# Block 0: conversions on ScalarE queued behind the Silu of an earlier chunk

## The chip, the cores and the metric

The kernel runs on one core of one Trainium2 chip. The metric is device time of one execution in microseconds; the kernel before took 980.23 us (median of 3 runs, 980.2 to 981.69). A core has five instruction queues that run in order each: TensorE (PE in the rows), VectorE (DVE), ScalarE (ACT), GpSimd (POOL) and SyncE (SP), which here issues the transfers. An instruction that waits holds up everything behind it in its own queue.

## The reference

```python
attn = softmax(scale * q @ k.T, masked)          # 4 batches, 8 heads, 576 positions, head size 64
                                                 # heads 0-3: the last 32 positions; heads 4-7: every 32nd
x = (attn @ v)  -> [2304, 512]
xn = x / sqrt(mean(x * x) + 1e-6) * rms_g
x = (silu(xn @ w_gate) * (xn @ w_val)) @ w_out   # [512,1536], [512,1536], [1536,512]
out = ((x @ w_a) * (x @ w_b)) @ w_out2           # the same sizes, other weights
```

All inputs and outputs are float32. Products are made as three matmuls on a high and a low part of each operand (hi*hi + hi*lo + lo*hi), so that every weight has to be converted into such a pair once, and every activation too.

## The kernel before, in words

The 2304 tokens are worked in six blocks of 384 (`t` = 0 to 5), and the hidden width of 1536 in twelve chunks of 128 (`fc` = 0 to 11). For each block and chunk, PE makes `g` and `v` (12 matmuls each, lines 478 to 480, of the block's normalised attention output `xx` with the chunk's pair `gv`), DVE scales `g` (line 750, tile `sg`), ACT applies Silu to it (line 751), DVE multiplies with `v` (line 761, tile `h`), ACT and POOL (or DVE) split `h` into its pair `hl` (lines 502 and 503), and one chunk later PE adds `h` times the output weights into four accumulators `y` (12 matmuls, same lines). `g` and `v` share three PSUM banks in turn. Block t+1's attention is worked between the chunks of block t: DVE and POOL make the strided heads (POOL products at lines 245 and 278, DVE sums at 248 and 281), and PE, ACT and DVE the local heads.

Block 0 has more to do: the weights come as raw 64-bit words and are converted here, chunk by chunk, one conversion being two steps on ACT (lines 134 and 139), one on DVE (142), a copy to the high part on ACT (147) and a subtraction for the low part on POOL (148). `convert1(fc + 1)` makes the gate and value weights of the next chunk (tiles `gv_raw`, `cz`, `gv`); another conversion, behind line 765, makes the output weights of this chunk (`raw` or `gv_raw`, a half as large `cz`, `wo`), which are then stored to DRAM (`wod`, line 767) for the blocks after. The small `cz` of the output weights has one buffer, so the next conversion's second step waits until POOL has made the low part of the one before. Chunk 11's gate and value words, and the output words of chunks 8 to 11, pass through a pool of two `raw` buffers (`load_late`): a load waits for DVE to have read what was in the buffer.

The order on each engine is not written out. The framework's scheduler lays instructions out by a timeline of its own and keeps data dependences; the source says only what may not be moved ahead of what: inside `with gate(n)` (lines 590 to 596) everything stays behind some steps of block 0's attention on the same engine, and `behind(list)` (lines 493 to 498), so far used for the last block, keeps what is traced inside it behind each listed instruction on the engine of that instruction.

Of the kernel before, what the change touches and what calls it, by code (L numbers as in the profile page):

```python
# [14 lines left out]
AF = mybir.ActivationFunctionType  # L15
# [59 lines left out]
def fused_kernel(ctx: ExitStack, tc: tile.TileContext, qtl, ktl, vl, qs, ks, vs, cst, w1, w2, out):  # L75
# [5 lines left out]
    nc = tc.nc  # L81

    def engine(c):
        return {"P": nc.gpsimd, "D": nc.vector}[c]
# [65 lines left out]
    def conversion(third, ready, pool, lo_eng, low, out=False):  # L150

        st = {}
        n = ready.shape[1] // 2

        def z():
            if not st:
                st["z"] = pool.tile([128, (1 if out else 2) * DM], U32, tag=f"cz{out}", name="cz", bufs=NCZ[out])
            return st["z"][:, :n * DM]

        def last():  # L160
            x = z().bitcast(F32).rearrange("p (a n) -> p a n", a=n)
            hl = ready.rearrange("p (a s) n -> p a s n", s=2)
            parts(x, hl[:, :, 0], hl[:, :, 1], lo_eng)

        return words(third, z, low=low) + [last]

    def run(steps):
        for f in steps:
            f()
# [312 lines left out]
    def mm_in(ps, w, sel, x):  # L482
        for cc in range(NCC):
            c = slice(cc * 128, (cc + 1) * 128)
            mm3(ps, w[:, sel, 0, c], w[:, sel, 1, c], x[cc][:, 0], x[cc][:, 1], cc == 0, cc == NCC - 1)

    def tmp(name):
        return act.tile([128, NTB], F32, tag="t", name=name, bufs=NTMP)

    made = []  # L490

    @contextmanager
    def behind(instructions):

        with ExitStack() as e:
            for i in instructions:
                e.enter_context(tc.issue_after(i))
            yield

    def split(h, lo_eng):  # L500
        hl = act.tile([128, 2, NTB], F32R, tag="hl", name="hl", bufs=3)
        made.append(nc.scalar.copy(hl[:, 0], h).ins)  # L502
        made.append(lo_eng.tensor_tensor(hl[:, 1], h, hl[:, 0].bitcast(F32), op=ALU.subtract).ins)  # L503
        return hl
# [26 lines left out]
    def load_units(n):  # L531
        for which in units[:n]:
            raw.update(zip(which, load_pair(w1, which)))
        del units[:n]

    def load_late(which):
        raw.update(zip(which, load_pair(w1, which, pool)))

    def convert1(fc):
        t = gv[fc] = gv_slot(F32R, "gv")  # L540
        two = [raw.pop((fc, k)) for k in range(2)]
        if fc in FUSEDW:
            both, ready = gvraw[fc], t.rearrange("p k a n -> p (k a) n")
            run(conversion(both.rearrange("p k a n -> p (k a) n"), ready, pool, engine(WLO[fc][0]), LOW[fc][0]))
        else:
            run(zipped(*(conversion(two[k], t[:, k], pool, engine(WLO[fc][k]), LOW[fc][k]) for k in range(2))))

    def wo_tile():
        return wop.tile([128, 2, DM], F32R, tag="wo", name="wo", bufs=3)
# [27 lines left out]
    @contextmanager  # L577
    def gate(fc):

        with ExitStack() as e:  # L580
            for key in GATES[min(fc, len(GATES) - 1)].split():
                e.enter_context(tc.issue_after(s0["st"][key].ins))
            yield
# [7 lines left out]
    def emit_y(t, fc):  # L591
        if fc == 0:
            for e in range(NCC):
                y[t, e] = psum.tile([128, 512], F32, tag=f"y{e}", name=f"y{e}")
        h = hl.pop((t, fc))
        w = wo.pop((t, fc))
        for e in range(NCC):
            c = slice(e * 128, (e + 1) * 128)
            mm3(y[t, e][:, :NTB], w[:, 0, c], w[:, 1, c], h[:, 0], h[:, 1], fc == 0, fc == NFC - 1)

    def evac_y(t):
        for e in range(NCC):
            ys = tmp("ys")
            nc.vector.tensor_tensor(ys, y[t, e][:, :NTB], ri[t], op=ALU.mult)
            nc.sync.dma_start(x2d[t, e // 2][:, e % 2], ys)

    def load_wo(t, fc):
        wt = wo[t, fc] = wo_tile()
        nc.sync.dma_start(wt.rearrange("p a n -> p (a n)").bitcast(F32), wod[fc])
# [4 lines left out]
    def attention_slot(steps, fc):  # L614
        st = steps["strided"]
        n_sl = 10
        part = st[len(st) * fc // n_sl:len(st) * (fc + 1) // n_sl] if fc < n_sl else []
        part += local[min(t, 1)].get(fc, "").split()
        part += ["rms", "rinv"] * (fc == n_sl)
        for n in part:  # L620
            steps[n]()
# [98 lines left out]
    for t in range(NB):  # L720
        if t == 1:
            apool.close()
            pool = apool.enter_context(tc.tile_pool(name="attn", bufs=1))
        if t == NB - 1:
            apool.close()
            cpool.close()
            pool = p2.enter_context(tc.tile_pool(name="forms", bufs=1, reuse_waits="tile"))
            early = [f for k in (4, 5, 0, 1, 2, 3) for f in convert_forms(k, k < 4)]
        nxt = attention(t + 1, pool, psum, itertools.cycle(["att"])) if t + 1 < NB else None
        x = [xt[t, cc] for cc in range(NCC)]  # L730
        for fc in range(NFC):
            if t > 0 and fc == 0:
                load_wo(t, 0)
            g_ps = psum.tile([128, 512], F32, tag="gv", name="g_ps", bufs=3)
            mm_in(g_ps[:, :NTB], gv[fc], 0, x)
            v_ps = psum.tile([128, 512], F32, tag="gv", name="v_ps", bufs=3)
            mm_in(v_ps[:, :NTB], gv[fc], 1, x)
            if t == 0 and fc + 1 < NFC:
                with gate(fc + 1):
                    convert1(fc + 1)  # L740
                if fc + 2 == NFC:
                    load_late([(NFC - 2, 2), (NFC - 1, 2)])
            if t == NB - 1:
                slab[fc] = wgt.tile([128, 4 * DM], F32 if fc in (0, 1, 11) else F32R, tag="gv", name="slab", bufs=NFC)
                with behind(made):
                    run(early[len(early) * fc // NFC:len(early) * (fc + 1) // NFC])
                    for k in [k for k in x0 if k <= fc]:
                        run(x0.pop(k))
            sg = tmp("sg")
            nc.vector.tensor_tensor(sg, g_ps[:, :NTB], ri[t], op=ALU.mult)  # L750
            nc.scalar.activation(sg, sg, AF.Silu)  # L751
            if fc == 1 and t > 0:
                evac_y(t - 1)
            if nxt is not None:
                attention_slot(nxt, fc)
            if prev is not None:
                emit_y(*prev)
            if t > 0 and fc + 1 < NFC:
                load_wo(t, fc + 1)
            h = tmp("h")  # L760
            made[:] = [nc.vector.tensor_tensor(h, sg, v_ps[:, :NTB], op=ALU.mult).ins]  # L761
            hl[t, fc] = split(h, engine(HLO0[fc] if t == 0 else HLO[t]))
            if t == 0:
                wt = wo[0, fc] = wo_tile()
                with gate(fc + 1):
                    run(conversion(raw.pop((fc, 2)), wt, pool, engine(WLO[fc][2]), LOW[fc][2], True))
                nc.sync.dma_start(wod[fc], wt.rearrange("p a n -> p (a n)").bitcast(F32))
                if fc % 2:
                    load_units(1)
                if fc == NFC - 3:  # L770
                    load_late([(NFC - 1, 0), (NFC - 1, 1)])
            prev = (t, fc)
# [240 lines left out]
```

## Time and profile before

| | |
|---|---|
| median of the runs | 980.23 us |
| profiled execution | 981.02 us |
| its span on the core | 979.2 us |
| PE busy | 949.2 us, 97% |
| DVE, ACT, POOL busy | 63%, 44%, 57% |
| mean granted clock of PE | 0.986 |

The span is from the first instruction to the last; 1.8 us of the profiled execution lie around it. PE has 30 us in which it does nothing, most of them in the first 160 us: the attention of block 0 up to 35 us, block 0's chunks from there to about 140 us. Matmuls of 384 columns start 0.17 us after each other at the full clock and overlap, so that a duration of 0.33 us is two of them. A row of the timeline gives the start, the busy time, the instruction, and in brackets how long its engine was idle before it and what ended that.

### The profile page before, as it was taken

The page shows a single profiled execution, that of the slowest core. Times are in us where ns is not written, and L with a number is a line of the kernel's source. Part 1 is how long each engine was busy: PE and PEld are TensorE (multiplying, and loading weights), DVE is VectorE, ACT ScalarE, POOL GpSimd, SP SyncE. Part 2 cuts the span into 40 slices and gives each one's busy share as a digit, 9 for nine tenths or more (in the row PEclk, how much of TensorE's full clock was granted, in tenths as well). Part 3 has the DMA queues.
Part 4 walks back from the last instruction along what each step waited for, and adds up shares of the span by engine and source line. Part 5 has one row for each costly group of instructions (what it writes and reads, how often), then busy time and mean ns, then how long its engine had stood idle before and what let it go on. Part 6 is the DMA issues. An engine that isn't in the chain of part 4 may idle for free.

```text
span 979.2 us, 14353 instructions
## 1 busy us (share of the span) xinstructions
PE 949.2 (97%) x5438; PEld 900.8 (92%) x5438; DVE 620.4 (63%) x891; ACT 427.7 (44%) x800; POOL 555.1 (57%) x418
## 2 busy tenths in 40 slices
PE   6899999999999999999999899999999999999998
PEld 5799989999999999999999899999999999999996
DVE  5568757638917984988565458667655655465534
ACT  4999645243534423433456455535434423122110
POOL 3489946558739776969468644754743424123211
PEclk7899999999999999999999999999999999999999
DMA  9963375435633643532687975897893973853701
GB/s 339 408 238 119 117 284 206 147 111 178 191 110 126 208 161 107 175 121 80 217 328 278 374 284 209 330 419 312 325 386 122 351 305 117 295 233 150 269 11 65
DMA packets 57364, 215.57 MB, mean 220 GB/s; under 512 B 5968, under 2 KB 14544, under 8 KB 51664
## 3 DMA queue, kind: packets, MB, share of 16 engines
q1 hardware_dynamic: 57296, 214.66, 59.7%
q8 instruction: 43, 0.70, 0.3%
q14 instruction: 25, 0.20, 0.1%
HBM read 172.17 MB, written 42.47 MB: 219 GB/s over the span
## 4 chain that ended last, share of the span: by engine, by line
PE 75%; DVE 6%; DMA 5%; POOL 5%; ACT 4%; issue 3%; SPq 1%; DVEq 0%; POOLq 0%; ACTq 0%
PE o L892 5%; PE o L894 5%; PE o L893 5%; PE Y L838 4%; PE Y L837 4%; PE Y L836 4%; PE y L478 3%; PE g_ps L478 3%; PE v_ps L478 3%; PE g_ps L480 3%; PE v_ps L480 3%; PE g_ps L479 3%; PE v_ps L479 3%; PE y L479 3%; PE y L480 3%
## 5 line engine op out<-in xcount | busy, mean ns | idle before, releaser
L148 POOL TENSOR_TENSOR hl<-c,hl 128x384 fp32r<-128x384 f32 x72 | 77.9, 1082 | 180.5 <-ACT hl L147 173.9
L245 POOL TENSOR_TENSOR prod<-kv_t,qs_t 128x512 f32<-128x512 f32 (+12 forms) x57 | 106.1, 1883 | 18.3 <-DMA kv_t<-in_ks 6.3
L503 POOL TENSOR_TENSOR hl<-h,hl 128x384 fp32r<-128x384 f32 x70 | 77.9, 1113 | 59.7 <-ACT hl L502 59.7
L478 PE MATMUL g_ps<-xx,gv 128*128 128x384 f32 x288 | 98.4, 342 | 5.1 <-DVE h L761 5.0
L478 PE MATMUL v_ps<-xx,gv 128*128 128x384 f32 x288 | 97.5, 339 | 3.5 <-DVE sg L750 3.0
L278 POOL TENSOR_TENSOR prod<-kv_t,S_t 128x512 f32<-128x512 f32 (+12 forms) x57 | 86.0, 1522 | 24.0 <-DVE S_t L270 7.7
L479 PE MATMUL y<-hl,wo 128*128 128x384 f32 x288 | 96.8, 341 | 1.3 <-POOL hl L503 1.3
L479 PE MATMUL v_ps<-xx,gv 128*128 128x384 f32 x288 | 97.8, 340 | 0.0
L480 PE MATMUL g_ps<-xx,gv 128*128 128x384 f32 x288 | 97.5, 339 | 0.0
L479 PE MATMUL g_ps<-xx,gv 128*128 128x384 f32 x288 | 97.3, 339 | 0.0
L480 PE MATMUL v_ps<-xx,gv 128*128 128x384 f32 x288 | 97.2, 338 | 0.0
L843 DVE TENSOR_TENSOR c<-c,Y 128x384 f32<-128x384 f32 x108 | 58.8, 551 | 58.6 <-PE Y L838 53.5
L480 PE MATMUL y<-hl,wo 128*128 128x384 f32 x288 | 95.4, 339 | 0.0
L281 DVE TENSOR_REDUCE xs_t<-prod 128x64 f32<-128x448 f32 (+17 forms) x57 | 85.2, 1515 | 6.0 <-POOL prod L278 5.8
L478 PE MATMUL y<-hl,wo 128*128 128x384 f32 x288 | 83.8, 343 | 2.8 <-DMA wo<-wod 1.8
L892 PE MATMUL o<-slab,hl 128*128 128x512 f32 x216 | 84.7, 393 | 1.0 <-DVE slab L901 0.5
L893 PE MATMUL o<-slab,hl 128*128 128x512 f32 x216 | 84.5, 392 | 0.0
L894 PE MATMUL o<-slab,hl 128*128 128x512 f32 x216 | 83.2, 394 | 0.0
L147 ACT CAST hl<-c 128x384 fp32r<-128x384 f32 x72 | 37.0, 514 | 94.2 <-DVE c L873 93.9
L751 ACT ACTIVATE sg<-sg 128x384 f32<-128x384 f32 x72 | 37.8, 525 | 87.6 <-DVE sg L750 78.0
L838 PE MATMUL Y<-slab,form 128*128 128x384 f32 x216 | 73.0, 338 | 0.0
L837 PE MATMUL Y<-slab,form 128*128 128x384 f32 x216 | 72.9, 338 | 0.0
(135 smaller groups left out, 2521.3 us busy)
## 6 DMA issues: line engine op xcount, KB each, us to landing
form<-formd SPq DMA_DIRECT2D x32, 1792.0 KB, 10.5
wo<-wod SPq DMA_DIRECT2D x60, 512.0 KB, 3.3
raw<-in_w SPq DMA_DIRECT2D x42, 512.0 KB, 7.4
gv_raw<-in_w SPq DMA_DIRECT2D x30, 512.0 KB, 10.0
formd<-form SPq DMA_DIRECT2D x6, 1792.0 KB, 7.0
formd<-forms SPq DMA_DIRECT2D x6, 1792.0 KB, 12.9
slab<-x2d SPq DMA_DIRECT2D x24, 384.0 KB, 4.5
wod<-wo SPq DMA_DIRECT2D x12, 512.0 KB, 3.4
```

The source lines that it names most:

```text
L148: lo_eng.tensor_tensor(lo, x, hi.bitcast(F32), op=ALU.subtract)
L245: nc.gpsimd.tensor_tensor(pr, st["ks", g][:, :, :n, :], st["qs"][:, heads(g), mm:mm + 1, :].to_broadcast([128, G, n, D]), op=ALU.mult)
L278: st["pvm"] = nc.gpsimd.tensor_tensor(pr, st["vs", g][:, :, :n, :], st["S"][:, heads(g), mm, :n, None].to_broadcast([128, G, n, D]), op=AL ...
L281: st["pvr"] = nc.vector.tensor_reduce(st["xs"][:, mm, heads(g), :], pr.rearrange("p g n d -> p g d n"), axis=X, op=ALU.add)
L478: nc.tensor.matmul(out_ps, w_hi, x_hi, start=start, stop=False)
L479: nc.tensor.matmul(out_ps, w_hi, x_lo, start=False, stop=False)
L480: nc.tensor.matmul(out_ps, w_lo, x_hi, start=False, stop=stop)
L837: nc.tensor.matmul(bank(n), hi, x[p][:, 1, c], start=False, stop=False, skip_group_check=not begins)
L838: nc.tensor.matmul(bank(n), lo, x[p][:, 0, c], start=False, stop=c == 1, skip_group_check=not begins)
L892: nc.tensor.matmul(o, h[:, 0, cols], w[0], start=n == 0, stop=False)
L893: nc.tensor.matmul(o, h[:, 0, cols], w[1], start=False, stop=False)
L894: nc.tensor.matmul(o, h[:, 1, cols], w[0], start=False, stop=n == len(chunks) - 1)
```

## The change

Two lines of block 0 get a further condition. The conversion of the gate and value weights of chunk n = `fc + 1` may not stand ahead of the Silu of chunk n - 4, and that of the output weights of chunk n not ahead of the Silu of chunk n - 2. Since the listed instruction is a Silu, this orders ACT's queue and no other; it adds no wait.

```diff
+    silu = {}
     made = []
...
             if t == 0 and fc + 1 < NFC:
-                with gate(fc + 1):
+                with gate(fc + 1), behind([silu[0, fc - 3]] if fc > 2 else []):
                     convert1(fc + 1)
...
             sg = tmp("sg")
             nc.vector.tensor_tensor(sg, g_ps[:, :NTB], ri[t], op=ALU.mult)
-            nc.scalar.activation(sg, sg, AF.Silu)
+            silu[t, fc] = nc.scalar.activation(sg, sg, AF.Silu).ins
...
             if t == 0:
                 wt = wo[0, fc] = wo_tile()
-                with gate(fc + 1):
+                with gate(fc + 1), behind([silu[0, fc - 2]] if fc > 1 else []):
                     run(conversion(raw.pop((fc, 2)), wt, pool, engine(WLO[fc][2]), LOW[fc][2], True))
```

The scheduler then lays out all engines anew, so that the order differs on each of them up to the first chunks of block 1. Three places are shown. First ACT's queue around the Silu of chunk 0 (`sg_452`; `gv_595` is chunk 3's pair, `gv_raw_185` chunk 4's words, `gv_raw_191` chunk 5's, `gv_raw_179` and `188` the output words of chunks 2 to 5). Before:

```order
L139 ACTIVATE cz_597<-gv_raw_182 128x1024
L134 ACTIVATE gv_raw_179<-gv_raw_179 128x512
L134 ACTIVATE gv_raw_185<-gv_raw_185 128x1024
L139 ACTIVATE cz_684<-gv_raw_185 128x1024
L134 ACTIVATE gv_raw_179<-gv_raw_179 128x512
L134 ACTIVATE gv_raw_188<-gv_raw_188 128x512
L139 ACTIVATE cz_650<-gv_raw_179 128x512
L134 ACTIVATE gv_raw_188<-gv_raw_188 128x512
L134 ACTIVATE gv_raw_191<-gv_raw_191 128x1024
L147 CAST gv_595<-cz_597 128x2x512
L751 ACT_TABLE_LOAD
L751 ACTIVATE sg_452<-sg_452 128x384
```

The same place in the changed kernel, as far as the split of `h` of chunk 0 (`hl_476`):

```order
L139 ACTIVATE cz_597<-gv_raw_182 128x1024
L147 CAST gv_595<-cz_597 128x2x512
L752 ACT_TABLE_LOAD
L752 ACTIVATE sg_452<-sg_452 128x384
L134 ACTIVATE gv_raw_179<-gv_raw_179 128x512
L139 ACTIVATE cz_650<-gv_raw_179 128x512
L134 ACTIVATE gv_raw_185<-gv_raw_185 128x1024
L139 ACTIVATE cz_684<-gv_raw_185 128x1024
L503 CAST hl_476<-h_474 128x384
```

Eight conversion steps that stood between `cz_597` and `gv_595` now stand behind the Silu, four of them still ahead of `hl_476`.

Second, POOL's queue in the last third of block 0, where the low part of chunk 7's output weights (`wo_1086`) is made; `wo_983` and `wo_1157` are those of chunks 6 and 8, `hl_1154` is the split of chunk 8, `prod` and `xx` belong to block 1's attention. Before:

```order
L503 TENSOR_TENSOR hl_1083<-h_1081,hl_1083 128x384
L278 TENSOR_TENSOR prod_1030<-kv_t_872,S_t_457 128x512
L396 TENSOR_TENSOR xx_1049<-x_t_1045,xx_1049 128x384
L148 TENSOR_TENSOR wo_1086<-cz_1088,wo_1086 128x512
L278 TENSOR_TENSOR prod_1033<-kv_t_872,S_t_457 128x640
L396 TENSOR_TENSOR xx_1066<-x_t_1061,xx_1066 128x384
L278 TENSOR_TENSOR prod_1133<-kv_t_872,S_t_457 128x768
L503 TENSOR_TENSOR hl_1154<-h_1152,hl_1154 128x384
L148 TENSOR_TENSOR wo_1157<-cz_1159,wo_1157 128x512
```

And in the changed kernel:

```order
L504 TENSOR_TENSOR hl_1083<-h_1081,hl_1083 128x384
L148 TENSOR_TENSOR wo_983<-cz_985,wo_983 128x512
L504 TENSOR_TENSOR hl_1154<-h_1152,hl_1154 128x384
L278 TENSOR_TENSOR prod_1033<-kv_t_872,S_t_457 128x640
L396 TENSOR_TENSOR xx_1049<-x_t_1045,xx_1049 128x384
L278 TENSOR_TENSOR prod_1133<-kv_t_872,S_t_457 128x768
L396 TENSOR_TENSOR xx_1066<-x_t_1061,xx_1066 128x384
L148 TENSOR_TENSOR wo_1086<-cz_1088,wo_1086 128x512
L396 TENSOR_TENSOR xx_1206<-x_t_1201,xx_1206 128x384
L396 TENSOR_TENSOR xx_1218<-x_t_1213,xx_1218 128x384
L148 TENSOR_TENSOR wo_1157<-cz_1159,wo_1157 128x512
```

The four instructions that stood right behind `wo_1086` (`prod_1033`, `xx_1066`, `prod_1133`, `hl_1154`) now stand ahead of it; up to `wo_1086` the two queues hold the same instructions otherwise.

Third, DVE in block 1, where the product of chunk 1 (`h_1525`) stands among the sums of block 2's attention (`S_t_1418`). Before:

```order
L248 TENSOR_REDUCE S_t_1418<-prod_1559 128x8
L248 TENSOR_REDUCE S_t_1418<-prod_1562 128x9
L311 SCALAR_TENSOR_TENSOR s_t_1579<-att_1502,cst_sb_113 128x384
L248 TENSOR_REDUCE S_t_1418<-prod_1567 128x7
L320 TENSOR_REDUCE lmx_1592<-s_t_1579 128x4
L761 TENSOR_TENSOR h_1525<-sg_1472,v_ps_1459 128x384
```

And in the changed kernel:

```order
L248 TENSOR_REDUCE S_t_1418<-prod_1559 128x8
L248 TENSOR_REDUCE S_t_1418<-prod_1562 128x9
L762 TENSOR_TENSOR h_1525<-sg_1472,v_ps_1459 128x384
L311 SCALAR_TENSOR_TENSOR s_t_1579<-att_1502,cst_sb_113 128x384
L248 TENSOR_REDUCE S_t_1418<-prod_1567 128x7
```

Here `h_1525` has moved ahead of three instructions.

## Rows read from the trace of the kernel before

**Rows 1.** Windows: stretch, length, busy us (instructions) of PE, PEld, DVE, ACT, POOL, clock.

```profile
41.50:60.48 18.98, 13.31 (x68) 12.68 (x67) 9.98 (x14) 18.95 (x28) 8.62 (x5) 0.91 0.98 382
60.48:117.25 56.77, 55.37 (x367) 52.93 (x366) 48.14 (x57) 46.30 (x91) 56.77 (x35) 1.00 0.31 108
117.25:132.00 14.75, 13.91 (x74) 12.39 (x73) 8.57 (x11) 13.01 (x23) 8.45 (x8) 1.00 0.66 239
```

**Rows 2.** Timeline of PE, 46 to 54 us.

```profile
46.02 0.34 PE L480 MATMUL v_ps<-xx,gv 128*128 128x384 f32 x1
51.07 0.69 PE L478 MATMUL g_ps<-xx,gv 128*128 128x384 f32 x1 [4.71 <-DVE h L761]
51.55 0.53 PE L479 MATMUL g_ps<-xx,gv 128*128 128x384 f32 x1
...
53.79 0.41 PE L480 MATMUL g_ps<-xx,gv 128*128 128x384 f32 x1
```

**Rows 3.** Timeline, ACT's and DVE's rows ahead of the first Silu.

```profile
47.55 1.04 ACT L147 CAST gv<-cz 128x1024 fp32r<-128x1024 f32 x1
...
49.90 0.52 ACT L751 ACTIVATE sg<-sg 128x384 f32<-128x384 f32 x1
...
42.30 1.16 DVE L142 SCALAR_TENSOR_TENSOR cz<-gv_raw,cz 128x1024 uint32<-128x1024 uint32 x1
```

**Rows 4.** Groups by shape, 36 to 132 us, ACT: count, busy us, mean ns.

```profile
L134 ACT ACTIVATE gv_raw<-gv_raw 128x1024 f32<-128x1024 f32 x8 | 9.2, 1145 | 0.0
L139 ACT ACTIVATE cz<-gv_raw 128x1024 uint32<-128x1024 uint16 x8 | 9.1, 1133 | 0.0
...
L139 ACT ACTIVATE cz<-gv_raw 128x512 uint32<-128x512 uint16 x7 | 4.7, 674 | 0.3 <-POOL wo L148 0.2
...
L134 ACT ACTIVATE gv_raw<-gv_raw 128x512 f32<-128x512 f32 x6 | 3.9, 687 | 0.0
```

**Rows 5.** Timeline of POOL, early in block 0 and around wo_1086.

```profile
48.67 2.34 POOL L148 TENSOR_TENSOR gv<-cz,gv 128x1024 fp32r<-128x1024 f32 x1 [7.17 <-ACT gv L147]
...
91.33 1.00 POOL L503 TENSOR_TENSOR hl<-h,hl 128x384 fp32r<-128x384 f32 x1
...
109.35 1.28 POOL L148 TENSOR_TENSOR wo<-cz,wo 128x512 fp32r<-128x512 f32 x1
...
114.68 1.33 POOL L503 TENSOR_TENSOR hl<-h,hl 128x384 fp32r<-128x384 f32 x1
```

**Rows 6.** Timeline of ACT, DVE, SP, PE: from wo_1157's conversion to chunk 11's v.

```profile
110.67 0.67 ACT L139 ACTIVATE cz<-raw 128x512 uint32<-128x512 uint16 x1 [0.15 <-POOL wo L148]
...
111.36 1.04 DVE L142 SCALAR_TENSOR_TENSOR cz<-raw,cz 128x512 uint32<-128x512 uint32 x1 [1.40 <-ACT cz L139]
...
112.43 0.33 SPq L108 DMA_DIRECT2D raw<-in_w  x1
...
126.06 0.45 PE L478 MATMUL v_ps<-xx,gv 128*128 128x384 f32 x1 [0.46 <-ACT gv L147]
```

**Rows 7.** Groups by shape, 36 to 132 us, POOL.

```profile
L148 POOL TENSOR_TENSOR gv<-cz,gv 128x1024 fp32r<-128x1024 f32 x9 | 24.5, 2720 | 12.2 <-ACT gv L147 12.2
...
L503 POOL TENSOR_TENSOR hl<-h,hl 128x384 fp32r<-128x384 f32 x9 | 12.5, 1391 | 3.1 <-ACT hl L502 3.1
```

**Rows 8.** Timeline of SP and of PE in block 1.

```profile
133.77 0.32 SPq L767 DMA_DIRECT2D wod<-wo  x1
...
144.36 0.44 PE L478 MATMUL v_ps<-xx,gv 128*128 128x384 f32 x1 [1.04 <-DVE sg L750]
...
150.88 1.13 PE L293 MATMUL att<-k_t,q_t 128*128 128x96 f32 x8 [1.14 <-DVE s_t L311]
...
152.32 0.44 PE L478 MATMUL g_ps<-xx,gv 128*128 128x384 f32 x1 [0.31 <-DVE h L761]
...
152.96 0.52 PE L478 MATMUL g_ps<-xx,gv 128*128 128x384 f32 x1
...
155.84 0.52 PE L478 MATMUL v_ps<-xx,gv 128*128 128x384 f32 x1
```

## The prediction

> **What bounds the kernel now.** I read the windows first: they show in which stretch which engine is full. Over the whole span PE is busy 97%, so that little more than its 30 us of idle time could ever be won, and a change in block 0 can touch only the idle time there. From 41.5 to 60.5 us ACT is full (18.95 of 18.98 us) while PE works 13.31 us; from 60.5 to 117.25 POOL has no idle time at all (56.77 of 56.77), and PE hardly any (55.37) [rows 1]. So block 0 has three stages: ACT sets the pace at first, then PE and POOL run level, and at the end something else does, since there POOL and ACT have idle time again (from 117.25 to 132, 6.3 and 1.7 us) [rows 1]. The timelines say what. At 51.07 PE has waited 4.71 us for `h` of chunk 0 [rows 2], which waits for the Silu at 49.90 [rows 3]; in ACT's queue eight conversion steps stand ahead of that Silu. At the end of block 0 a chain decides: the second step of chunk 8's output conversion waits for POOL's low part of chunk 7's (`wo_1086`, ending 110.63), DVE then reads the raw words (to 112.40), that frees the buffer, SP loads chunk 11's gate words at 112.43, and chunk 11's `v` starts on PE at 126.06 after a wait of 0.46 us [rows 5, 6]. PE arrives there just in time. A second wait stands in block 1: 1.04 us at 144.36, then 1.14 and 0.31 before 152.32, on DVE [rows 8].
>
> **The change, part by part.**
>
> *The first wait.* The copy `gv_595` starts at 47.55 before, though DVE's step that it needs ended at 43.46 (42.30 + 1.16) [rows 3]. Now nothing stands between them: copy, table load, Silu and `h` come 4.09 us earlier, and `h` is there at 46.9 instead of 51.0. PE's wait of 4.71 us [rows 2] shrinks to 0.6. Behind the wait the matmuls took 0.53 us instead of 0.34, until 53.79 [rows 2]: the granted clock was at 1.2 GHz, and nine matmuls came 0.32 us apart instead of 0.17, 1.3 us lost. A wait of 0.6 us should not bring that. So PE is 4.1 + 1.3 = 5.4 us ahead of its old time at chunk 2. This is what the change removes, and were PE alone in charge afterwards, it would be the answer.
>
> *What is moved behind.* ACT has the same work: what is no longer ahead of the Silu is ahead of something else. Four steps now stand between Silu 0 and the split `hl_476`: about 0.67 + 0.69 + 1.15 + 1.13 us by their means [rows 4], less 0.1 for each where they overlap, 3.2 us. POOL starts with `gv_595` at 44.6 instead of 48.67 [rows 5], 4.1 us earlier, but is through at 46.9 and then has nothing until `hl_476` is copied at 50.1. Carried on down ACT's new list in the same way, by the means of its shapes, POOL is without work for 3.2, 1.5, 0.8, 0.6, 1.2 and 2.7 us before it runs through from 66, 10.0 in sum (the last is the softmax of block 1's first local heads, whose normalisation now stands in POOL's queue ahead of two products). Before, from 48.67 to 60.48, it was idle for 11.81 - 8.62 = 3.2 us [rows 1, 5]. With 6.8 more idle time and a start 4.1 earlier POOL is 2.7 us later at equal work. The means carried so far put ACT some 0.7 us later than a count of its work does, so I take 2.0, with 0 and 4 as ends.
>
> *The queue past which `wo_1086` is moved.* Four instructions now stand ahead of it; before, they stood right behind it and took from 110.63 to 116.01, 5.4 us [rows 5]. POOL is full there, so they count whole: `wo_1086` ends at 110.63 + 2.0 + 5.4 = 118.0. Chunk 8's conversion, the buffer, SP's load and chunk 11 hang on it as before [rows 6], 7.4 us later: `v` of chunk 11 starts at 133.5 instead of 126.06. PE, 5.4 us ahead at chunk 2, loses that in waits on the way (for POOL's low parts from chunk 7 on, for chunk 11's gate words, and for these) and 7.4 more. What is left to do behind this point is the same in both.
>
> How far POOL's list stretches is the least certain size here. In this trace the 1024-wide low parts take 2.34 us at best [rows 5] and 2.72 on the mean, the splits 1.00 at best and 1.39 on the mean [rows 5, 7]; of the six such low parts and five splits from 60.5 to 110.6 that makes 6 x 0.38 + 5 x 0.39 = 4.2 us. I take it that the new list is stretched as much, since DVE has as much to do beside it. If nothing stretched, `wo_1086` would end 4.2 earlier, and the shift would be 3.2 instead of 7.4.
>
> The Trainium skill, "SBUF — State Buffer", section "Who interferes with whom", says that a VectorE instruction with two SBUF inputs contends with a GpSimd instruction that reads SBUF, by a lock that is held for a whole instruction. The spread of the rows just named [rows 7] is in line with that. By this rule the stretch stays, as two-input instructions on VectorE are as many as before; a sum without it would be 0.7 where mine below is 4.9.
>
> *What is given back in block 1.* The wait before 152.32 ends with DVE's sums for block 2's attention, whose loads stand in SP's queue behind the store of chunk 11's output weights, at 133.77 [rows 8]; that is 21.3 us behind the load at 112.43 [rows 6]. In the new order DVE converts chunk 11's output words before it is held by the block's reciprocal and the `sg` of chunk 11, by my walk 18.5 us behind that load: 2.8 us less. `h_1525` also moves ahead of three DVE instructions, and `sg_1472` ahead of a sum, so it no longer waits for that. So the waits of 1.04, 1.14 and 0.31 go, 2.5 us, and with them the low clock behind: from 152.96 to 155.84 ten matmuls came 0.32 us apart instead of 0.17 [rows 8], 1.5 us. Together 4.0, as long as nothing else is late there; 0 if the chain behind chunk 11 keeps its length.
>
> *A new low clock.* PE will wait about 3 us for chunk 11's `g` and 2 us for its `v`, close together. Rows 2 and 8 show the clock at 1.2 GHz behind waits in sum of 4.7 and of 2.5 us; each cost 1.3 to 1.5 us. I take 1.5, with 0 and 3 as ends. Nothing else hides or adds: no instruction and no table load is added, the same bytes are loaded, and from block 1's chunk 3 on the work is the same.
>
> **Sum.** +7.4 - 4.0 + 1.5 = +4.9 us, the 5.4 of the first part being lost on the way. On the profiled execution's 981.02 us (span 979.2, 1.8 around it) that is 985.9; the median of the runs is 0.8 below the profiled execution, so I forecast 985.1 us. With the ends of the terms its own range is 980.5 to 990.
>
> **The rivals.**
>
> *Faster: POOL keeps up.* If POOL's early idle time is only what it was (0 instead of 2.0, or less still, as the products are fed earlier) and its rows stretch by 4.2 us less, then chunk 11's words come 1 to 3 us later instead of 7.4, and the 4.0 us in block 1 are still won: 980.2 + 2 - 4 = 978, and 975 if the four moved instructions find room too. It decides from where `wo_1086` ends before 113.5. For it: POOL has 6.3 us of idle time behind 117.25 [rows 1]. Against it: POOL's full window [rows 1], and that the four instructions are ahead of `wo_1086` whatever their durations.
>
> *No change.* With a shift of 3 to 5 us, the gain in block 1 and the loss at chunk 11 cancel: 980 us. The bounds above allow it in the lower third.
>
> *Slower than forecast: nothing is given back.* If the chain behind chunk 11 keeps its 21.3 us and DVE's new order only moves the wait, the end is 7.4 + 1.5 later: 989. For it: all of block 1's first sums hang on the same SP queue [rows 8].
>
> *The change does not act.* The new condition orders a queue that the scheduler is free to arrange; it is excluded by the order, in which Silu 0 has moved ahead of eight steps.
>
> **How the numbers follow.** The forecast gets 0.46, nothing given back 0.16, no change 0.17, faster 0.20, and 0.01 is left to the last. About 0.2% (2 us) can be told from no change here, so faster means below 978.3, slower above 982.2. Of the forecast and the case of nothing given back nearly all is slower; a little of the forecast falls below 982.2, as much of the case of no change above: slower 0.62, same 0.18, faster 0.20. The range for 8 in 10 reaches from inside the faster case, 976.5, to past the slow one, 989.5.
>
> **What would show it.** In the changed profile PE's wait for `h` near 46 us should be under 1 us, with the clock at its higher level behind it. POOL should be idle for several stretches between 47 and 66. `wo_1086` should end near 118, the load of chunk 11's gate words be issued near 120, and `v` of chunk 11 start near 133.5, with waits of PE of 2 to 3 us for the copies of chunk 11's pair. The waits on DVE in block 1, at 144 and 152, should be gone or below 1 us. I am wrong if the load is issued before 116, if PE is ahead of its old time when block 1 begins, or if waits stand in a place that I have not named.

## The result, and the profile after

The changed kernel takes 985.91 us (median of 4 runs, 984.91 to 987.71), the kernel before 980.22 beside it (978.5 to 981.69): ratio 1.0058, 95% interval 1.0046 to 1.007. It is slower by 5.7 us. The profiled span grew by the same amount within its spread, from 979.2 to 984.1 us, at a mean granted clock of 0.986 in both.

Windows of the changed kernel, the stretches and columns of [rows 1]:

```profile
41.50:60.48 18.98, 17.37 (x101) 16.73 (x100) 11.65 (x14) 17.26 (x24) 11.54 (x6) 1.00 0.96 376
60.48:117.25 56.77, 51.26 (x318) 47.81 (x318) 44.77 (x56) 45.07 (x89) 49.74 (x32) 0.94 0.25 89
117.25:132.00 14.75, 10.62 (x49) 9.33 (x48) 8.04 (x10) 11.29 (x21) 6.84 (x6) 0.88 0.58 213
```

In the first stretch PE works 4.1 us more than before, in the second 4.1 less, in the third 3.3 less. POOL, which had no idle time in the second stretch, now has 7.0 us, 3.8 of them before 66 us.

PE's waits of over 0.5 us from 46 us on (timeline of PE, changed kernel; the columns are those of [rows 2]):

```profile
46.48 0.45 PE L478 MATMUL g_ps<-xx,gv 128*128 128x384 f32 x1 [0.66 <-DVE h L762]
...
84.89 1.11 PE L354 MATMUL att<-cst_sb,s_t 128*96 128x128 f32 x8 [2.65 <-ACT pt L365]
...
101.18 0.69 PE L478 MATMUL g_ps<-xx,gv 128*128 128x384 f32 x1 [2.17 <-DVE h L762]
...
104.72 0.52 PE L479 MATMUL y<-hl,wo 128*128 128x384 f32 x1
105.05 0.52 PE L478 MATMUL y<-hl,wo 128*128 128x384 f32 x1
...
120.99 0.88 PE L441 MATMUL att<-sq,ones 128*128 128x384 f32 x2 [1.30 <-DVE sq L435]
...
126.81 0.44 PE L478 MATMUL g_ps<-xx,gv 128*128 128x384 f32 x1 [2.83 <-ACT gv L147]
...
132.89 0.38 PE L478 MATMUL v_ps<-xx,gv 128*128 128x384 f32 x1
...
155.34 0.44 PE L478 MATMUL g_ps<-xx,gv 128*128 128x384 f32 x1 [0.54 <-DVE h L762]
...
178.28 0.98 PE L354 MATMUL att<-cst_sb,s_t 128*96 128x128 f32 x7 [0.85 <-DVE s_t L345]
...
180.61 0.45 PE L479 MATMUL y<-hl,wo 128*128 128x384 f32 x1 [1.07 <-POOL hl L504]
...
185.62 1.14 PE L354 MATMUL att<-cst_sb,s_t 64*64 64x64 f32 x16 [0.74 <-ACT pt L365]
```

The wait of 4.71 us [rows 2] is 0.66 now. In its place stand 2.65 and 2.17 in the middle and 1.30 and 2.83 around chunk 11, and behind 2.17 matmuls come 0.32 us apart (104.72, 105.05): the clock was at 1.2 GHz. The waits of [rows 8] are gone but for 0.54, and three others have come at 178 to 186.

To compare kernels I add up, for four stretches, PE's idle time (gaps over 0.15 us) and what the low clock cost: each matmul of lines 478 to 480 that starts 0.26 to 0.4 us behind the one before it without a wait counts with what it exceeds 0.168. In us, worked out from the rows of each trace:

| kernel | 38 to 60.5 | 60.5 to 108 | 108 to 138 | 138 to 200 | sum |
|---|---|---|---|---|---|
| before | 5.67 + 1.18 | 1.05 + 0.56 | 0.92 + 0.34 | 2.50 + 2.29 | 14.5 |
| changed | 1.61 + 0.23 | 5.51 + 2.62 | 4.13 + 2.01 | 3.20 + 0.57 | 19.9 |
| difference | -5.0 | +6.5 | +4.9 | -1.0 | +5.4 |

The difference of 5.4 us accounts for the 4.9 us of the spans within 0.5. So the early Silu gave 5.0 us; the middle of block 0 took more than that back; 4.9 us went at its end.

The chain at that end, changed kernel, timelines of DVE, POOL, ACT and SP (columns as in [rows 6]):

```profile
112.17 0.55 DVE L762 TENSOR_TENSOR h<-sg,v_ps 128x384 f32<-128x384 f32 x1 [2.28 <-PE v_ps L480]
...
113.34 1.50 DVE L142 SCALAR_TENSOR_TENSOR cz<-gv_raw,cz 128x512 uint32<-128x512 uint32 x1
...
114.87 0.62 ACT L147 CAST wo<-cz 128x512 fp32r<-128x512 f32 x1 [1.91 <-DVE cz L142]
...
115.57 1.29 POOL L148 TENSOR_TENSOR wo<-cz,wo 128x512 fp32r<-128x512 f32 x1 [1.28 <-ACT wo L147]
...
118.64 0.68 ACT L139 ACTIVATE cz<-raw 128x512 uint32<-128x512 uint16 x1
...
119.34 1.04 DVE L142 SCALAR_TENSOR_TENSOR cz<-raw,cz 128x512 uint32<-128x512 uint32 x1 [0.41 <-ACT cz L139]
...
120.41 0.33 SPq L108 DMA_DIRECT2D raw<-in_w  x1
```

`wo_1086` (115.57) is released by ACT and not by POOL's own queue: POOL was through with the instructions ahead of it at 114.29 and waited 1.28 us for ACT's copy, that for DVE's step, and this stood behind an `h` that waited 2.28 us for PE itself. Then chunk 8's second step (118.64) starts 1.8 us behind `wo_1086`'s end, since it stands behind a Silu and four other steps in ACT's queue, where before it followed at once [rows 6].

### The profile page after: what moved, and what is told of

The parts are those of the page before. It is cut to its first block, busy times and chain, and to the rows that moved or that the text cites. A ratio compares the mean times of both kernels' runs of the same rounds, so it can differ in the third digit from the quotient of the medians.

```text
span 984.1 us, 14362 instructions
## 1 busy us (share of the span) xinstructions
PE 949.5 (96%) x5438; PEld 900.0 (91%) x5438; DVE 620.5 (63%) x891; ACT 427.2 (43%) x800; POOL 550.6 (56%) x418
## 4 chain that ended last, share of the span: by engine, by line
PE 67%; DVE 6%; DMA 4%; POOL 3%; issue 3%; ACT 2%; SPq 0%; DVEq 0%; POOLq 0%; ACTq 0%
PE o L893 5%; PE o L895 5%; PE o L894 5%; PE Y L839 4%; PE Y L838 4%; PE Y L837 4%; PE y L478 3%; PE v_ps L478 3%; PE y L479 3%; PE y L480 3%; PE v_ps L480 3%; PE v_ps L479 3%; PE Z L839 3%; PE Z L838 3%; PE Z L837 3%
## 5 line engine op out<-in xcount | busy, mean ns | idle before, releaser
L504 POOL TENSOR_TENSOR hl<-h,hl 128x384 fp32r<-128x384 f32 x70 | 75.2, 1074 | 65.5 <-ACT hl L503 58.5
```

## The experiments

In the first four kernels the scheduler lays out the variant anew; in the others a list holds the order. Sums are those of the table above.

**A third buffer for the late words.** Theory A: the late load of chunk 11's words is the loss. Rival B: PE's waits in the middle are.

```diff
-        return pool.tile([128, 2, DM], U32, tag="raw", name="raw", bufs=2)
+        return pool.tile([128, 2, DM], U32, tag="raw", name="raw", bufs=3)
...
-            x_t = piece("xr", "x_t", 4)
+            x_t = piece("xr", "x_t", 2 if t == 1 else 4)
```

In the changed kernel (a_raw3): 

> The changed kernel with a third raw buffer (room for it from two instead of four x_t buffers in block 1's attention), so that chunk 11's gate words need not wait until chunk 8's output words have been read. Theory A (the 5.7 us are lost because these words come 8 us later): the load is issued before 100 us, chunk 11's g and v no longer wait, PE keeps most of the 4.6 us that it is ahead at chunks 0 to 5, and the time is 974 to 979. Rival B (POOL and ACT run out earlier, the waits of PE at 85 and 101 us are the loss, the words are only late with the rest): 983 to 986.

In the kernel before (b_raw3): 

> The kernel before with the same third raw buffer. The wait of 4.7 us for the first Silu stays. Theory A: chunk 11 was on time already but for 0.46 us, so little comes of it by itself, 1 to 3 us by the earlier end of chunk 11's conversions: 977 to 980. Rival B: no change, 980. The difference to the changed kernel with the same buffer is what the earlier Silu is worth: A 2 to 5 us in favour of the changed one, B 3 to 6 against it.

Measured: 981.48 us, ratio 1.0008 (0.9999 to 1.0017), and 984.47, ratio 1.0033 (1.002 to 1.0045). Both theories missed both times, and in a_raw3 the late load stands at 104.35, not before 100; the difference between the two, 3.0 us in favour of the early Silu, is in theory A's range. The scheduler laid out the whole block anew, and PE waited elsewhere: the sums are 15.0 and 19.0 us. What the pair shows is that the sign of the change hangs on the order around it.

**One condition at a time** (without the other `behind(...)`).

Gate and value weights only (a_gv_only): 

> Only the first condition (gate and value conversions behind the Silu of four chunks earlier). In the order chunk 8's output conversion stands behind ten Silus, between nine before and eleven in the changed kernel. Theory A: the load of chunk 11's words is issued between 113 and 120 us, and the time goes with it: 979 to 984. Rival B: ACT's steps ahead of Silu 0 are fewer than before by half, so PE's first wait and the later ones lie between the two kernels: 981 to 984, whatever the time of that load.

Output weights only (a_wo_only): 

> Only the second condition (output conversions behind the Silu of two chunks earlier). In the order chunk 8's output conversion stands behind eleven Silus, as in the changed kernel, and ahead of the raw words of chunk 11 that of chunk 9 too. Theory A: the load is issued at 118 to 121 us, the time is 983 to 988. Rival B: between the two kernels, 981 to 984.

Measured: 982.97 us, ratio 1.0018 (1.0008 to 1.0027), within both; and 979.25, ratio 0.9985 (0.9972 to 0.9998), outside both. In a_wo_only the load stands at 116.89, 4.5 us later than before [rows 6], and PE waits 3.55 us near there, and yet it is the fastest of all kernels here; from 138 to 200 us PE waits nowhere. Timelines of SP and PE of a_wo_only:

```profile
116.89 0.33 SPq L108 DMA_DIRECT2D raw<-in_w  x1
...
124.18 0.69 PE L478 MATMUL y<-hl,wo 128*128 128x384 f32 x1 [3.55 <-ACT wo L147]
```

So theory A fell: a late load alone doesn't decide. To go on without the scheduler's new layouts, I held the order fixed. The trace order of the instructions is the same in both kernels, so a list can give each engine the order of either, or a part of each:

```diff
         fused_kernel(tc, *args)
+        hold_order(tc, nc.cur_bb.bb.instructions)   # each instruction behind its predecessor in ORDER
```

**The changed order up to 66 us, then the old one (h_a66); up to 108 us, then the old one (h_a108).**

> The kernel before with the order of every engine held by a list: what the changed kernel starts before 66 us stands in the changed kernel's order, everything else in the order of the kernel before. So Silu 0 comes early, and from chunk 4 on the old order follows. Theory A (ScalarE is full from 42 to about 100 us in either kernel, so the 4 to 5 us that PE gains at chunk 0 are only lent, and come back as waits of PE for ScalarE's results between 66 and 107): waits of PE of 3 us or more in sum between 66 and 107, time 978 to 982. Theory B (the middle is harmless, the loss is made by the late words of chunk 11 alone): with the old order there the words come by 114 at the latest, the lead of PE is kept, 974 to 977. If the early order itself costs (POOL's idle time, as predicted): load near 115, 982 to 985.

> The changed kernel's order on every engine up to 108 us, behind it the order of the kernel before. Waits of PE at 85, 92 and 101 us as in the changed kernel by construction. Theory A (half of the loss is made in the middle): the end of block 0 is repaired in part only, 981 to 984. Theory B (the loss is the order behind 108 us: chunk 8's output conversion behind Silu 10, and the load that hangs on it): load issued by 116, 977 to 980. If the order behind 108 us plays no part: 984 to 987.

Measured: 983.7 us, ratio 1.0029 (1.0018 to 1.0041), and 981.74, ratio 1.0013 (0.9998 to 1.0028). In h_a66 the lead is gone by 77 us (timeline of PE):

```profile
73.20 0.44 PE L480 MATMUL y<-hl,wo 128*128 128x384 f32 x1 [1.87 <-POOL wo L148]
...
76.57 0.74 PE L354 MATMUL att<-cst_sb,s_t 128*96 128x128 f32 x2 [2.75 <-DVE s_t L311]
```

Its sums are 1.9, 7.6, 2.3 and 5.4: the middle costs nearly as much under the old order as under the new one (7.6 and 8.1), so the lead isn't lost to the new order there. In all thirteen kernels of this document the first two sums together are 8.3 to 14.5 us (8.5 before): no order tried here kept the lead up to 108 us. That it is lost in the middle was theory A's point, but its time was 1.7 us too low: the third case holds, the load (116.30) came 3.9 us later than before [rows 6], and the time is in its 982 to 985. In h_a108 the front and the middle are those of the changed kernel (1.8, 6.6), the end is 2.8 in place of 6.1. Ratios 1.0058 against 1.0013: the order behind 108 us is worth some 4.4 us (1.8 to 7 by the two intervals). The load stood at 115.62, as theory B had it, and the time in theory A's 981 to 984: part of the loss is the end's order, part was made before.

**Three conversion steps moved from ACT to DVE (a_lowd), the same in the kernel before (b_lowd)**, each order held.

```diff
-LOW = ["AAA"] * NFC
+LOW = ["DAA" if f in (7, 8, 9) else "AAA" for f in range(NFC)]
```

> The changed kernel with its order held by a list, but the second conversion step (line 139) of the gate and value words of chunks 7, 8 and 9 is a shift on VectorE, right ahead of VectorE's own step, in place of the step on ScalarE: 3 x 1.13 us less on ScalarE between 72 and 92 us. Theory A (ScalarE ends PE's waits in the middle): the waits of 2.65, 0.5 and 2.17 us at 85, 92 and 101 us fall to under 2 in sum, and the time to 977 to 981. Theory B (only POOL and the late words of chunk 11 count): the waits move to chunk 11, 983 to 986.

> The kernel before with its order held by a list and the same three conversion steps on VectorE in place of ScalarE. Theory A: PE waits for ScalarE only at chunk 0 (4.7 us) there and once later (1.05 us at 88), which the three steps at 68, 76 and 84 us hardly touch: 978.5 to 981, while the changed kernel gains 4 to 7 us by the same edit. Theory B: no change either, 979 to 981.

Measured: 988.83 us, ratio 1.0084 (1.007 to 1.0097), and 984.73, ratio 1.0038 (1.0023 to 1.0053): both slower, which neither theory had (the changed kernel was to gain, or to stay). DVE's groups of a_lowd by shape, 60 to 110 us (count, busy us, mean ns):

```profile
L142 DVE SCALAR_TENSOR_TENSOR cz<-gv_raw,cz 128x1024 uint32<-128x1024 uint32 x5 | 10.4, 2078 | 2.0 <-ACT cz L139 1.7
...
L136 DVE TENSOR_SCALAR cz<-gv_raw 128x1024 uint32<-128x1024 uint32 x3 | 4.2, 1389 | 0.0
```

A step that takes 1.16 us alone [rows 3] takes 2.08 here, and PE's wait at 87.43 (2.33 us) ends on DVE's `h`. That `h` (86.84) stands in DVE's queue right behind a moved step of 2.06 us and DVE's own of 2.66 us: DVE has idle time in that stretch, but not where these steps stand.

**The three first steps on ACT left out (a_act_less, and b_act_less from the kernel before)**, each order held, nothing added elsewhere.

```diff
-            nc.scalar.activation(y, y, AF.Prelu, scale=-2.0 ** -80, alpha=-2.0 ** -32)
+            if low != "S":
+                nc.scalar.activation(y, y, AF.Prelu, scale=-2.0 ** -80, alpha=-2.0 ** -32)
...
-            nc.vector.scalar_tensor_tensor(z(), raw[:, :, 1], 3, z(), op0=ALU.logical_shift_left, ...
+            nc.vector.scalar_tensor_tensor(z(), raw[:, :, 1], 0 if low == "S" else 3, z(), op0=...
```

> The changed kernel with its order held by a list, without the first conversion step (line 134, ScalarE, 1.15 us each) of the gate and value words of chunks 7, 8 and 9; VectorE's step shifts by 0 in place of 3 there, so that the numbers stay finite. 3.4 us less on ScalarE between 72 and 86 us, and nothing added on any other engine; the weights of three chunks are left without their scaling, so the result is another one. Theory A (ScalarE ends PE's waits in the middle, and the move to VectorE failed only because VectorE's steps got longer beside POOL): the waits of 2.65, 0.5 and 2.17 us between 84 and 102 us fall to under 2.5 in sum, chunk 11's gate words are loaded 2 to 3 us earlier, time 980 to 983. Rival (ScalarE isn't what holds PE there, VectorE and POOL are): waits stay at 4 us or more, 984.5 to 987.

> The kernel before with its order held by a list, without the same three steps on ScalarE (at 67, 75 and 82 us there; the same part of the result is left out). PE waits only 1.05 us between 60 and 126 us there. Theory A: at most that wait goes, 978.5 to 981. Rival (ScalarE's work counts one to one in either kernel): 975.5 to 977.5.

> The same kernel as the one before it in this list that leaves out three steps on ScalarE in the changed kernel, for its trace (the profiled execution of the first time took 5266 us, against 984.4 to 986.9 us of the others, and can't be read). Its times say that 3.4 us less on ScalarE give 1 to 1.5 us: 984 to 985.5 again. If PE is held by the conversions as a whole, the idle time of PE between 60 and 108 us falls from 5.5 us by less than 2, and its waits end on VectorE and POOL in place of ScalarE; if ScalarE alone held it, that idle time falls by 3 or more and the loss has moved behind 108 us.

Measured: 984.71 us, ratio 1.0045 (1.0031 to 1.0058; the execution of 5266 us, whose cause is not known, is left out); before with the edit 980.9, ratio 0.9998 (0.9989 to 1.0007); the first again 985.17, ratio 1.0046 (1.0033 to 1.0058). So 3.4 us less on ACT give the changed kernel some 1.2 us, in both runs (the intervals with and without the edit overlap), and the kernel before nothing, so that there theory A's range holds and its rival is out. The wait for ACT in the middle fell from 2.65 to 0.58 us, but another came behind it; timelines of PE and POOL of the last run (its lines are one higher):

```profile
82.35 1.11 PE L355 MATMUL att<-cst_sb,s_t 128*96 128x128 f32 x8 [0.58 <-ACT pt L366]
...
86.77 0.69 PE L481 MATMUL g_ps<-xx,gv 128*128 128x384 f32 x1 [2.16 <-POOL gv L149]
...
84.38 5.13 POOL L149 TENSOR_TENSOR gv<-cz,gv 128x1024 fp32r<-128x1024 f32 x2
```

The idle time from 60.5 to 108 us fell from 5.5 to 4.2: that is the rival's case, of the conversions as a whole and not of ACT alone, and theory A's time of 980 to 983 was wrong. Behind 108 us 1.2 us of the gain were lost again (a sum of 7.3 in place of 6.1).

**Block 1's new order by itself (h_t164)**: the order of before, but from 136 to 164 us that of the changed kernel.

> The kernel before with the order of every engine held by a list: the order of before up to 136 us, then the changed kernel's order for what that starts by 164 us (block 1's first chunks, with h_1525 ahead of three instructions of VectorE), then the order of before again. If the waits of 1.04, 1.14 and 0.31 us and the low clock behind them (1.5 us) hang on the order in block 1 alone: 976 to 978, faster than both kernels. If they hang on the loads behind the store of chunk 11's output weights, which stay where they were: 979.5 to 981.

Measured: 980.83 us, ratio 1.0001 (0.9992 to 1.001). The sum of 138 to 200 us is 4.8, as before: the waits of 1.14 and 0.31 us [rows 8] become 0.69, that at 144 stays (1.24), and two others come. That is the second case, of the loads that stay where they were, or of a pace that is set elsewhere. Timeline of PE of h_t164:

```profile
150.92 0.44 PE L478 MATMUL g_ps<-xx,gv 128*128 128x384 f32 x1 [0.69 <-DVE h L761]
...
174.78 0.44 PE L479 MATMUL y<-hl,wo 128*128 128x384 f32 x1 [0.69 <-POOL hl L503]
...
180.74 0.44 PE L354 MATMUL att<-cst_sb,s_t 64*64 64x64 f32 x4 [1.53 <-ACT pt L365]
```

**All sums beside all times.** The change of the sum against before, and the change of the time by the ratio: changed +5.4 and +5.7 us; a_raw3 +0.4, +0.8; b_raw3 +4.5, +3.2; a_gv_only +2.8, +1.8; a_wo_only +1.5, -1.5; h_a66 +2.7, +2.8; h_a108 +0.9, +1.3; a_lowd +7.7, +8.2; b_lowd +4.9, +3.7; a_act_less_again +5.0, +4.5; b_act_less +0.7, -0.2 (in these two, lines 479 to 481 are counted); h_t164 0.0, +0.1. Eleven of the twelve agree within 1.3 us, so the time goes with PE's idle time and clock up to 200 us. a_wo_only is off by 3.0. Of these, 0.8 lie between the profiled span, 0.7 us shorter than before, and the median; some 1.2 are time that PE's other matmuls (the attention's), whose pace the sum doesn't count, took less from 38 to 200 us; the rest stays open.

## Why the prediction came out, step by step

The time came out 0.8 us from the forecast, and the places of the loss in part. Step by step:

*The first wait: right.* 0.66 us measured, 0.6 said, the clock at 1.00 behind it; 5.0 us gained, 5.4 said.

*PE's lead is lost on the way: right in sum, wrong in place.* I put it to POOL's low parts from chunk 7 on and to chunk 11. It went from 85 us on, in waits that end on ACT and DVE, and cost 6.5 us with the low clock. By my own signs that is a miss: the waits at 85 and at 178 to 186 us stand in places that I had not named. `h` was 4.6 us ahead at chunk 0 and 5.0 at chunk 3 (65.83 before, 60.80 after). At chunk 7 it is level, and at chunk 8 it is 5.4 ahead again; DVE's timelines, before:

```profile
100.42 0.54 DVE L761 TENSOR_TENSOR h<-sg,v_ps 128x384 f32<-128x384 f32 x1
...
109.43 0.54 DVE L761 TENSOR_TENSOR h<-sg,v_ps 128x384 f32<-128x384 f32 x1
```

And changed, with the step ahead of chunk 7's `h`:

```profile
97.49 3.17 DVE L142 SCALAR_TENSOR_TENSOR cz<-gv_raw,cz 128x1024 uint32<-128x1024 uint32 x1 [1.29 <-ACT cz L139]
100.59 0.54 DVE L762 TENSOR_TENSOR h<-sg,v_ps 128x384 f32<-128x384 f32 x1
...
104.05 0.56 DVE L762 TENSOR_TENSOR h<-sg,v_ps 128x384 f32<-128x384 f32 x1 [0.64 <-ACT sg L752]
```

So a single `h` doesn't tell how far PE is ahead, since the order on PE differs too; the sums do. What holds PE in the middle is shown in part only. Behind the wait of 2.17 us at 101.18 stands a long DVE step: the Silu of chunk 7 ended at 99.29 and PE's matmuls of `v` before that, but `h` waited for the step that ran from 97.49 to 100.66, 2.0 us longer than alone [rows 3], so some 1.3 us of that wait are its stretch. h_a66 shows that the old order doesn't keep the lead either, a_act_less that relief on ACT passes the wait to POOL, and a_lowd that more steps on DVE make it longer. That no single engine sets the pace there fits all three; what would have kept the lead stays open.

*POOL's early idle time: right.* 8.7 us in six stretches between 46 and 66 us (the longest 3.01 ahead of `hl_476`), 10.0 said.

*POOL 2.0 us later, then a queue of four that counts whole: the queue held, the 2.0 failed.* POOL's timelines, before and then changed (the split of chunk 7's `h`, and the last instruction ahead of `wo_1086`):

```profile
106.06 1.02 POOL L503 TENSOR_TENSOR hl<-h,hl 128x384 fp32r<-128x384 f32 x1
```

```profile
106.15 1.00 POOL L504 TENSOR_TENSOR hl<-h,hl 128x384 fp32r<-128x384 f32 x1
...
113.04 1.25 POOL L396 TENSOR_TENSOR xx<-x_t,xx 128x384 fp32r<-128x384 f32 x1
```

At this split POOL is 0.1 us later than before, not 2.0 (the next step says why), and from 66 to 114.29 it was idle for 1.5 us only. By its own queue `wo_1086` would have ended at 115.6, 4.9 us later than before, for 5.4 said. The 1.28 us of waiting for ACT's copy, behind the late PE, I had not priced. So it ended at 116.86, 6.2 us later; I had said 118.0.

*POOL stretches as before: this failed.* POOL's groups by shape, 36 to 132 us, changed kernel, beside [rows 7]:

```profile
L148 POOL TENSOR_TENSOR gv<-cz,gv 128x1024 fp32r<-128x1024 f32 x9 | 23.3, 2585 | 8.6 <-ACT gv L147 8.6
...
L504 POOL TENSOR_TENSOR hl<-h,hl 128x384 fp32r<-128x384 f32 x9 | 9.7, 1082 | 5.1 <-ACT hl L503 4.6 <-POOL wo L148 0.6
```

They lost 4.0 us (24.5 + 12.5 against 23.3 + 9.7), and POOL's busy time over the whole span fell from 555.1 to 550.6. DVE as a whole didn't get them: its busy time is 620.4 and 620.5. Within DVE the stretch moved between instructions. Its groups by shape, same stretch, before and then changed:

```profile
L142 DVE SCALAR_TENSOR_TENSOR cz<-gv_raw,cz 128x1024 uint32<-128x1024 uint32 x9 | 12.1, 1342 | 3.9 <-ACT cz L139 3.9
...
L435 DVE TENSOR_TENSOR sq<-sq 128x384 f32<-128x384 f32 x3 | 3.6, 1211 | 2.5 <-ACT sq L429 2.5
...
L270 DVE TENSOR_TENSOR S_t<-S_t,srs 128x72 f32<-128x72 f32 x1 | 2.1, 2146 | 0.0
```

```profile
L142 DVE SCALAR_TENSOR_TENSOR cz<-gv_raw,cz 128x1024 uint32<-128x1024 uint32 x8 | 14.6, 1830 | 4.5 <-ACT cz L139 3.1 <-DMA k_t<-in_ktl 1.3
...
L435 DVE TENSOR_TENSOR sq<-sq 128x384 f32<-128x384 f32 x3 | 1.9, 627 | 0.0
...
L270 DVE TENSOR_TENSOR S_t<-S_t,srs 128x72 f32<-128x72 f32 x1 | 0.2, 232 | 0.0
```

Eight conversion steps took 0.49 us more each, 3.9 us; two other groups took 3.7 less. That counts, since the conversion steps stand ahead of an `h` for which PE waits, as at 97.49.

*Chunk 11: right in time, from other parts.* The load came at 120.41 (about 120 said), 8.0 us later than before where I had 7.4. But I let chunk 8's conversion hang on `wo_1086` "as before", and it stood behind a Silu and four steps of ACT: 6.2 us from `wo_1086`, 1.8 from there. That these come near 2.0 + 5.4 is luck. `v` started at 132.89 (133.5 said), without the wait that I had put there; PE waited 2.83 us for `g` and 1.30 ahead of an attention matmul. h_a108 confirms that the order behind 108 us carries most of the loss: without it some 4.4 of the 5.7 us are gone.

*Given back in block 1, 4.0 us: mis-sized, it is 1.0.* The waits went as said, and the store of chunk 11's output weights came 18.4 us behind the load (138.76, 18.5 said). But 0.85, 1.07 and 0.74 us came at 178 to 186, where I had said that the work is the same; h_t164 shows that this order alone gives nothing.

*The low clock at chunk 11, +1.5 us: right,* 1.7 more from 108 to 138 us. The 1.0 less at the front and the 1.7 less in block 1 are in the terms above; the 2.1 more in the middle I had not named.

So the sum, +4.9, was met in part by luck, by two errors against each other: too much given back (3.0 us), and too much lost up to 138 us, where I had 7.4 + 1.5 and the table has 6.4 (-5.0 + 6.5 + 4.9). Of the rivals, "nothing given back" was nearer in mechanism than its time of 989 tells. "Faster" is out: `wo_1086` would have had to end before 113.5.

## What to carry to other kernels

A wait that goes at the head of a stretch is worth something only if the engines that feed the waiting one can run faster afterwards: follow them through the stretch, sum up the waiting engine's idle time there instead of comparing single rows, and price the waits that the lead turns into, with the low clock behind them. Waits that a new order removes in the next block are counted as gained only when nothing as late stands behind them; holding the order fixed and changing one stretch at a time tells these apart, where an edit that lets the scheduler lay out everything anew does not. The version with the output weights' condition alone is the only one here below the kernel before, by 0.15% with an interval of 0.02 to 0.28%.

## What the runs showed of the hardware

Either engine can pay for a collision of VectorE and GpSimd. Timelines of the changed kernel, DVE and then POOL:

```profile
82.01 2.82 DVE L142 SCALAR_TENSOR_TENSOR cz<-gv_raw,cz 128x1024 uint32<-128x1024 uint32 x1
...
79.96 3.79 POOL L245 TENSOR_TENSOR prod<-kv_t,qs_t 128x640 f32<-128x640 f32 x2
83.71 3.37 POOL L148 TENSOR_TENSOR gv<-cz,gv 128x1024 fp32r<-128x1024 f32 x1
```

DVE's step starts inside POOL's product and ends at 84.83, 1.08 us behind the product's end at 83.75, about its own 1.16 us [rows 3]: as if it had not moved until then. POOL's next instruction, started at 83.71, ends 2.25 us behind DVE's end, near its best time of 2.34 [rows 5]. In the kernel before the same step runs at its own time inside a POOL instruction of 4.00 us, 1.66 more than POOL's best (DVE, POOL):

```profile
77.38 1.20 DVE L142 SCALAR_TENSOR_TENSOR cz<-gv_raw,cz 128x1024 uint32<-128x1024 uint32 x1
...
76.85 4.00 POOL L148 TENSOR_TENSOR gv<-cz,gv 128x1024 fp32r<-128x1024 f32 x1
```

The Trainium skill, "SBUF — State Buffer", section "SBUF: two separate sides", says that of a VectorE instruction with two SBUF inputs and a GpSimd instruction that reads SBUF, whichever starts first has the shared ports for its whole instruction and the other fully blocks. The changed kernel's rows agree. In those of before POOL's row begins 0.53 us ahead of DVE's and yet it is POOL that took longer, so the starts in the rows alone don't tell who will wait; why, stays open. The prediction took the stretch as POOL's alone; by these rows it falls to either.
